# Chunk-selecting attention and a squared-ReLU feed-forward layer on one core: the first token tile of every batch taken ahead of the rest, the rest in parts of two and three tiles, and the order written as named steps

## Chip, cores and metric

The kernel runs on one core of one Trainium2 chip. The metric is the device time of one execution in microseconds, as the median of several runs. Everything below about times comes from those runs or from one profiled execution of the kernel before.

## The reference, cut to what matters

Inputs are q, k and v of shape (4 batches, 8 heads, 768 tokens, 64), and the weights `moe_w_in` (512 x 2048) and `moe_w_out` (2048 x 512), all in float32. Keys are grouped in 24 chunks of 32 tokens.

```python
k_min, k_max = min and max of each chunk of k, by element
ub = np.sum(np.maximum(q * k_min, q * k_max), axis=-1)   # per query and chunk
ub = np.where(causal, ub, -1e9)
top_chunks = the 6 chunks with the largest ub
scores = q @ k.T / 8, where the key's chunk is selected and key <= query, else -1e9
attn = softmax(scores); out = attn @ v
x = out with heads side by side, 3072 x 512
h = np.maximum(x @ w_in, 0.0)
return h * h @ w_out                                     # 3072 x 512
```

A query in the first 128 tokens has at most four causal chunks, so for this tile the choice of six selects all of them.

## The kernel before, in words

Everything is computed in bf16 with float32 accumulation. The work is cut into 32 slots: `slots` runs over batch, half of the sequence (384 tokens, three tiles of 128) and head pair. "A" below is the first half of a batch (`half == 0`) and "B" the second. For each slot a fixed set of steps is issued:

- `step_P` makes `qr`, the negative and positive part of the transposed queries (VectorE), and for some slots the chunk minima and maxima (`extrema`; for later halves `step_K` does it once for all head pairs with a chain of halving minima or maxima).
- `step_U` multiplies `qr` by the chunk extrema (`kbd`) on TensorE to get the bounds `ub`, finds the six largest with `nc.vector.max`, and writes `nsel`, a mask of chunks not selected.
- `step_V` transposes `nsel` and copies it into the free half of the rows of `qc`. The keys hold a one-hot code of their chunk times -2^24 in the matching rows, so one matmul of 128 rows gives scores with unselected chunks pushed far down.
- `step_E` does the score matmuls (`ps`, L358) and the exponential on ScalarE (`e`, L363); a select on GpSimd (L367) clears the part above the diagonal.
- `step_F` multiplies by v with a column of ones (`po`, L383), takes the reciprocal and writes `x`.

After a half has all its `x`, `step_X` transposes it (on TensorE or with DMA transposes) and puts that half's feed-forward work in `queue`: 16 "ups" (`ffn_up`: four matmuls of 128x384 into `ph`, a ReLU on ScalarE or VectorE into `ht`, a square on VectorE into `h`) and 12 "downs" (`ffn_down`: four matmuls of 128x512 into `py`; after the fourth down of a tile, a copy to `ob` and a store). `fill` takes items from `queue` between the attention steps, by a quota for each slot. The order of all instructions is the order in which the Python code issues them (`manual_schedule`); each engine works through its own list in that order.

Batch 0's first half is special. Its q and k are staged in float32 in 16 DMAs, cast, and transposed on TensorE (`step_cast`, `step_T0`); no feed-forward work exists until `step_X(0, True)`. Its second half and batch 1's first half are transposed on TensorE in `step_T1` and placed by DMA (`place`); later halves use DMA transposes (`tr`). Loads that cast to bf16 are issued from GpSimd (`load_n`, `load_s`, `load_v`, `load_w`, `load_wo`) at slots listed in `later`.

The PSUM pools that matter: `psS` with 3 buffers (scores), `psF` with 2 (`ph`), `psY` with 1 (`py`), `psA` with 2 (`ub`, `qt`, `po`, `pt`).

Of the kernel before, what the change touches and what calls it, by code (L numbers as in the profile page):

```python
# [15 lines left out]

CH = 32
TOPK = 6
HT = 3
HB = HT * 128  # L20
NEG = -1.0e9
OFFSEL = -float(2 ** 24)

BANKS = (
    (((0, 0, 0, 3), (384, 2, 2, 1)), ((256, 1, 1, 2),)),
    (((0, 3, 3, 3), (384, 5, 5, 1)), ((0, 0, 3, 2), (256, 4, 4, 2)),
     ((0, 0, 5, 1), (128, 1, 3, 3)), ((0, 2, 3, 3),)),
)  # L30


@with_exitstack
def kernel(
# [12 lines left out]
    NT = S // 128  # L47
# [4 lines left out]
    NFI = DFF // 128  # L52
    scale = 1.0 / (D ** 0.5)
# [8 lines left out]
    vn = [consts.tile([128, H, NT, D + 1], BF16, tag=f"vn{i}", name="vn") for i in range(2)]  # L62
# [3 lines left out]
    QROW = (D, 0)  # L66
    SROW = (0, D)
    kcs = [[consts.tile([128, NP, S], BF16, tag=f"kc{i}_{h}", name="kc") for h in range(2)]
           for i in range(2)]
    qcs = [consts.tile([128, NP, 2, HB], BF16, tag=f"qc{i}", name="qc") for i in range(2)]  # L70


    qn0 = consts.tile([128, HT, NP, 4, D], BF16, tag="qn0", name="qn")

    nsel = [consts.tile([128, HT, 2, D], BF16, tag=f"ns{i}", name="nsel") for i in range(3)]
    kbds = [consts.tile([128, NP, 2, 2, NC], BF16, tag=f"kbd{i}", name="kbd")
            for i in range(2)]
# [3 lines left out]
    def load_n(n, b, j):  # L81
        t = nat[n, b, j] = work.tile([128, DM], BF16, tag=f"{n}n", bufs=7, name=f"{n}n")
        nc.gpsimd.dma_start(  # L83
            out=t.rearrange("p (h d) -> p h d", d=D),
            in_=(q if n == "q" else k)[b, :, 128 * j:128 * (j + 1)]
            .rearrange("h p d -> p h d"))

    def load_s(n, b, half):

        t = nat[n, b, half] = work.tile([128, H, HT, D], BF16, tag=f"{n}s", name=f"{n}s")  # L90
        nc.gpsimd.dma_start(
            out=t.rearrange("p h j d -> p h (j d)"),
            in_=(q if n == "q" else k)[b, :, HB * half:HB * (half + 1)]
            .rearrange("h (p j) d -> p h (j d)", j=HT))

    def load_v(b, h0, h1, j0, j1):
        if j1 - j0 == 1:
            nc.gpsimd.dma_start(
                out=vn[b % 2][:, h0:h1, j0, 0:D],
                in_=v[b, h0:h1, 128 * j0:128 * j1].rearrange("h p d -> p h d"))  # L100
        else:
            nc.gpsimd.dma_start(
                out=vn[b % 2][:, h0:h1, :, 0:D],
                in_=v[b, h0:h1].rearrange("h (j p) d -> p h j d", p=128))


    staged = []

    def stage(p, pool):
        t = []  # L110
        for eng, src in ((nc.sync, k), (nc.scalar if p < 2 else nc.sync, q)):
            x = pool.tile([128, HT, 2, D], F32, tag=f"st{len(t)}", bufs=NP, name="stage")
            for hh in range(2):
                eng.dma_start(
                    out=x[:, :, hh, :],
                    in_=src[0, 2 * p + hh, 0:HB].rearrange("(j p) d -> p j d", p=128))
            t.append(x)
        staged.append(t)

    ctx.enter_context(tc.manual_schedule())  # L120
    early = ExitStack()
    epool = early.enter_context(tc.tile_pool(name="early", bufs=NP))
    for p in range(NP):
        stage(p, epool)
# [3 lines left out]
    cmask = consts.tile([128, HT, 2, NC], BF16, tag="cmask", name="cmask")  # L128
    nc.vector.memset(cmask, 0.0)
    ident = consts.tile([128, 128], BF16, tag="ident")  # L130
    make_identity(nc, ident)
# [4 lines left out]
    for g in range(4):  # L136
        nc.gpsimd.affine_select(
            out=cmask[g * 32:(g + 1) * 32], in_=cmask[g * 32:(g + 1) * 32],
            compare_op=ALU.is_ge, fill=NEG,
            base=12 + g, channel_multiplier=0,  # L140
            pattern=[[4, HT], [0, 2], [-1, NC]])

    hmask = consts.tile([128, 2, 2, 12], BF16, tag="hmask")
    nc.vector.memset(hmask, 0.0)
    for r in range(2):
        nc.vector.memset(hmask[64 * r:64 * r + 64, 0, r, :], -1.0)
        nc.vector.memset(hmask[64 * r:64 * r + 64, 1, r, :], 1.0)

    nc.vector.memset(qn0[:, :, :, 0, :], 0.0)
    nc.vector.memset(qn0[:, :, :, 3, :], 0.0)  # L150
    nc.vector.memset(vn[0][:, :, :, D:D + 1], 1.0)

    for h in range(2):
        nc.vector.tensor_copy(
            kcs[0][h][SROW[h]:SROW[h] + D, :, 0:HB],
            oneh[:, 0:HB].unsqueeze(1).to_broadcast([D, NP, HB]))
    warm = consts.tile([128, 1], F32, tag="warm")
    nc.scalar.activation(warm, hmask[:, 0, 0, 0:1], ACT.Exp)

    def codes(i, p, c0):  # L160
        for h in range(2):
            nc.sync.dma_start(
                kcs[i][h][SROW[h]:SROW[h] + D, p, c0:S], oneh[:, c0:S])

    def clear(i):
        nc.vector.memset(nsel[i][:, :, :, 12:D], 0.0)
        if i == 0:
            nc.vector.memset(vn[1][:, :, :, D:D + 1], 1.0)
# [4 lines left out]
    def col_of(half, j, i):  # L173
        for n, bank in enumerate(BANKS[half]):
            for (at, jj, i0, m) in bank:
                if jj == j and i0 <= i < i0 + m:
                    return 512 * n + at + 128 * (i - i0)
        raise KeyError

# [3 lines left out]
    kbd = {}  # L183


    def step_cast(p):
        t = staged[p]
        kst = work.tile([128, HT, 2 * D], BF16, tag="kst", name="kst")
        nc.vector.tensor_copy(kst.rearrange("p j (h d) -> p j h d", h=2), t[0])
        nc.scalar.copy(qn0[:, :, p, 1:3, :], t[1])  # L190
        st[p] = {"kst": kst}

    def extrema(kt, s):

        b, half, p = slots[s]
        km = work.tile([128, 2, 12], BF16, tag="km", name="km")
        kv = kt.rearrange("p (c j) -> p c j", j=CH)
        nc.vector.tensor_reduce(km[:, 0, :], kv, axis=AX.X, op=ALU.min)
        nc.vector.tensor_reduce(km[:, 1, :], kv, axis=AX.X, op=ALU.max)
        nc.vector.tensor_mul(  # L200
            kbds[b % 2][:, p, :, :, 12 * half:12 * half + 12], hmask,
            km.unsqueeze(2).to_broadcast([128, 2, 2, 12]))

    def step_T0(s):

        p = s
        t = st[s]
        tk = psF.tile([128, HB], BF16, tag="ph", name="tk")
        tq = psF.tile([128, HB], BF16, tag="ph", name="tq")
        for j in range(HT):  # L210
            nc.tensor.matmul(tk[:, 128 * j:128 * (j + 1)], lhsT=t["kst"][:, j, :],
                             rhs=ident, is_transpose=True, start=True, stop=True)
# [11 lines left out]
    def step_T0b(s):  # L224
        nc.scalar.copy(kcs[0][1][0:D, s, 0:HB], st[s]["tk"][D:128])
# [437 lines left out]
```

## Time and profile before

| | |
|---|---|
| median of 3 runs | 285.89 us (285.44 to 286.31) |
| profiled execution, its own time | 286.44 us |
| profiled execution, span from first to last instruction | 284.7 us |
| TensorE (PE) busy | 258.8 us, 91% of the span, 2360 matmuls |
| weight loads (PEld) | 159.8 us, 56% |
| VectorE (DVE) busy | 170.0 us, 60% |
| ScalarE (ACT) busy | 179.9 us, 63% |
| GpSimd (POOL) busy | 83.9 us, 29% |
| mean granted TensorE clock | 0.981 |
| DMA | 33.32 MB in 105423 packets, mean 117 GB/s |

Busy time of TensorE is the time in which at least one matmul was under way. It includes the filling and draining of the pipeline, so a stretch can be shown as fully busy while fewer columns pass than the engine could take. The table is a mean over stages with different limits; the prediction reads it stage by stage.

### The profile page before, as it was taken

The page shows a single profiled execution, that of the slowest core. Times are in us where ns is not written, and L with a number is a line of the kernel's source. Part 1 is how long each engine was busy: PE and PEld are TensorE (multiplying, and loading weights), DVE is VectorE, ACT ScalarE, POOL GpSimd, SP SyncE. Part 2 cuts the span into 40 slices and gives each one's busy share as a digit, 9 for nine tenths or more (in the row PEclk, how much of TensorE's full clock was granted, in tenths as well). Part 3 has the DMA queues.
Part 4 walks back from the last instruction along what each step waited for, and adds up shares of the span by engine and source line. Part 5 has one row for each costly group of instructions (what it writes and reads, how often), then busy time and mean ns, then how long its engine had stood idle before and what let it go on. Part 6 is the DMA issues. An engine that isn't in the chain of part 4 may idle for free.

```text
span 284.7 us, 6484 instructions
## 1 busy us (share of the span) xinstructions
PE 258.8 (91%) x2360; PEld 159.8 (56%) x2360; DVE 170.0 (60%) x639; ACT 179.9 (63%) x370; POOL 83.9 (29%) x125
## 2 busy tenths in 40 slices
PE   1768779987988999999999999999999999999994
PEld 1546456644655566664565566655555666555543
DVE  6767688746797566744775377644865453342321
ACT  4586678765865777765668577756767677534410
POOL 8445131544155115721461116610211011000000
PEclk9975999999999999999999999999999999999999
DMA  8999999999999555995699629995424010101002
GB/s 158 173 217 179 219 202 166 165 173 157 92 132 177 57 96 67 194 166 129 78 202 106 119 60 122 187 165 127 122 78 58 37 39 0 39 37 39 37 37 74
DMA packets 105423, 33.32 MB, mean 117 GB/s; under 512 B 90928, under 2 KB 101424, under 8 KB 105392
## 3 DMA queue, kind: packets, MB, share of 16 engines
q0 software_dynamic: 63264, 12.85, 62.4%
q1 hardware_dynamic: 40528, 19.67, 32.4%
q10 hardware_dynamic: 1600, 0.39, 0.6%
q8 instruction: 18, 0.29, 0.4%
q14 instruction: 13, 0.11, 0.1%
HBM read 27.26 MB, written 6.29 MB: 118 GB/s over the span
## 4 chain that ended last, share of the span: by engine, by line
PE 74%; DVE 8%; ACT 7%; DMA 5%; issue 2%; SPq 1%; POOL 1%; ACTq 0%; POOLq 0%
PE py L457 26%; PE ph L438 25%; PE ps L358 11%; PE po L383 7%; DMA stage<-in_q_dram 4%; ACT ht L445 2%; ACT e L363 2%; DVE h L447 2%; PE ub L308 2%; DMA xT<-x 1%; PE tkq L260 1%; DVE x L393 1%; ACT qc L345 1%; PE qt L339 1%; ACT ob L464 1%
## 5 line engine op out<-in xcount | busy, mean ns | idle before, releaser
L363 ACT ACTIVATE e<-ps 128x512 bf16<-128x512 f32 x192 | 96.9, 549 | 24.9 <-PE ps L358 23.4
L438 PE MATMUL ph<-xT,w_in 128*128 128x384 bf16 x512 | 101.6, 325 | 2.6 <-DVE ht L443 0.8
L457 PE MATMUL py<-w_out,h 128*128 128x512 bf16 (+1 forms) x400 | 98.6, 371 | 3.8 <-DVE h L447 3.0
L447 DVE TENSOR_TENSOR h<-ht 128x384 bf16<-128x384 bf16 x128 | 47.8, 377 | 73.0 <-ACT ht L445 72.5
L445 ACT ACTIVATE ht<-ph 128x384 bf16<-128x384 f32 x120 | 59.0, 494 | 40.8 <-PE ph L438 38.8
L367 POOL TENSOR_SCALAR_AFFINE_SELECT e<-e 128x384 bf16<-128x384 bf16 x64 | 33.6, 526 | 157.4 <-ACT e L363 157.4
L438 PEld LDWEIGHTS <-w_in 128*128 128x128 bf16 x512 | 47.2, 97 | 32.8 <-issue 4.7
L358 PE MATMUL ps<-qc,kc 128*128 128x384 bf16 (+2 forms) x320 | 58.7, 287 | 2.5 <-DVE qc L334 1.0
L457 PEld LDWEIGHTS <-h 128*128 128x128 bf16 x400 | 37.0, 98 | 35.9 <-DVE h L447 6.4
L358 PEld LDWEIGHTS <-kc 128*128 128x128 bf16 x320 | 27.6, 100 | 18.1 <-issue 2.4
L383 PEld LDWEIGHTS <-e 128*128 128x128 bf16 x672 | 26.5, 100 | 6.9 <-POOL e L367 1.9
L383 PE MATMUL po<-vn,e 128*128 128x65 bf16 x672 | 28.3, 196 | 1.3 <-POOL e L367 1.2
L315 DVE MAX8 m<-ub 128x8 f32<-128x24 f32 (+1 forms) x160 | 16.6, 171 | 8.4 <-PE ub L308 8.3
L464 ACT COPY ob<-py 128x512 f32<-128x512 f32 x19 | 11.3, 593 | 11.5 <-PE py L457 11.3
L393 DVE TENSOR_TENSOR x<-po,r 128x384 bf16<-128x384 f32 x32 | 17.8, 558 | 1.1
L308 PE MATMUL ub<-kbd,qr 128*128 128x48 bf16 (+1 forms) x160 | 9.8, 182 | 4.0 <-ACT qr L218 1.6
L83 POOL DMA_DIRECT2D kn<-in_k_dram x15 | 13.3, 886 | 0.3 <-issue 0.3
L83 POOL DMA_DIRECT2D qn<-in_q_dram x15 | 13.3, 889 | 0.0
L344 DVE COPY qc<-qt 64x384 bf16<-64x384 bf16 (+1 forms) x28 | 8.9, 317 | 6.9 <-PE qt L339 6.9
L265 ACT COPY tT<-tkq 128x768 bf16<-128x768 bf16 x8 | 11.6, 1449 | 2.1 <-PE tkq L260 2.0
L283 DVE TENSOR_TENSOR km<-km 128x384 bf16<-128x384 bf16 (+3 forms) x40 | 11.6, 291 | 1.4
L308 PEld LDWEIGHTS <-qr 128*128 128x128 bf16 x160 | 7.6, 98 | 6.3 <-ACT qr L218 2.5
(67 smaller groups left out, 173.4 us busy)
## 6 DMA issues: line engine op xcount, KB each, us to landing
out_dram<-ob SPq DMA_DIRECT2D x23, 256.0 KB, 2.3
vn<-in_v_dram POOLq DMA_DIRECT2D x6, 384.0 KB, 8.9
w_in<-in_moe_w_in_dram POOLq DMA_DIRECT2D x2, 1024.0 KB, 11.5
w_out<-in_moe_w_out_dram POOLq DMA_DIRECT2D x2, 1024.0 KB, 12.5
kn<-in_k_dram POOLq DMA_DIRECT2D x15, 128.0 KB, 5.6
qn<-in_q_dram POOLq DMA_DIRECT2D x15, 128.0 KB, 7.0
kc<-tT SPq DMA_DIRECT2D x10, 192.0 KB, 6.0
qc<-tT SPq DMA_DIRECT2D x10, 192.0 KB, 7.4
```

Of the source, the lines that this page charges most:

```text
L83: nc.gpsimd.dma_start(out=t.rearrange("p (h d) -> p h d", d=D), in_=(q if n == "q" else k)[b, :, 128 * j:128 * (j + 1)] .rearrange("h p d ...
L308: nc.tensor.matmul(ub[:, j - j0], lhsT=st[s]["qr"][:, w, 128 * j:128 * (j + 1)], rhs=kbds[b % 2][:, p, w, :, 0:ncs], start=False, stop=(j ...
L315: nc.vector.max(out=m8[:, j, hh, :], in_=ub[:, j - j0, hh, :])
L358: nc.tensor.matmul(ps[:, at:at + 128 * m], lhsT=kcs[b % 2][hh][:, p, 128 * j:128 * (j + 1)], rhs=qcs[half][:, p, hh, c:c + 128 * m], start ...
L363: nc.scalar.activation(e[:, 512 * n + lo:512 * n + hi], ps[:, lo:hi], ACT.Exp, scale=float(scale))
L367: nc.gpsimd.affine_select(out=d, in_=d, compare_op=ALU.is_ge, fill=0.0, base=0, channel_multiplier=-1, pattern=[[0, 3], [1, 128]])
L383: nc.tensor.matmul(po[:, hh, i, :], lhsT=t["e"][hh][:, c:c + 128], rhs=vn[b % 2][:, 2 * p + hh, j, :], start=(j == 0), stop=(j == iq))
L393: nc.vector.tensor_mul(x[:, :, 128 * p:128 * (p + 1)].rearrange("p j (h d) -> p h j d", h=2), po[:, :, :, 0:D], r.to_broadcast([128, 2, HT ...
L438: nc.tensor.matmul(ph[:, 0:HB], lhsT=w_in[:, ki, 128 * f:128 * (f + 1)], rhs=xT[:, ki, :], start=(ki == 0), stop=(ki == NKI - 1))
L445: nc.scalar.activation(ht, ph[:, 0:HB], ACT.Relu)
L447: nc.vector.tensor_mul(h, ht, ht)
L457: nc.tensor.matmul(py[t][:, n0:n1], lhsT=h2[hb, f][:, 128 * t:128 * (t + 1)], rhs=w_out[:, f, n0:n1], start=(f == 0), stop=(f == NFI - 1))
```

## The change

The token tiles of a batch are no longer split 3 + 3. The first tile (tokens 0 to 127, called z here) is taken for all four batches at the very beginning and without any selection: the steps `z_cast`, `z_T`, `z_E`, `z_F`, `z_X` compute plain causal attention for it, with matmuls over 64 rows and a triangle of -2^24 (`tri`) added by a matmul. The rest of a batch is a part A of two tiles and a part B of three (`T0`, `NTP`). The feed-forward work has ten blocks instead of eight: two blocks of two z tiles each, then A and B of each batch. An up of a z or A block has matmuls of 256 columns, one of a B block 384.

A part A slot has three exponentials instead of four, because both heads share banks (`BANKA`); a part B slot keeps its eight. The q and k of batch 0 are loaded with whole groups of tokens contiguous per partition (`load_p`, and `stage` for the z tiles), and are transposed by `spread`: sixteen matmuls of 64 columns against pieces of the identity. Later halves still use DMA transposes (`tr`).

Feed-forward work is chosen by `pick` from two lists, `ups` and `downs`, that run over all blocks: a down is taken when its four `h` are at least five items old, and ups and downs alternate; at most 37 `h` tiles are alive (`HCAP`). `fill` spends a budget of columns per slot. The order of the steps is written as text: `PRELUDE` before the slots, and for each kind of slot a line of `SLOTS`. Names: `f` spends a share of the budget on ups or downs, `fu` on ups alone, `up.n` spends n x 512 columns on ups, `idle.n` does n matmuls whose result nobody reads, `go` issues the DMAs that are due, `KB` and `K` are the extrema, `T` a batch-0 transpose.

```diff
-HT = 3
-HB = HT * 128
+T0 = (1, 3)
+NTP = (2, 3)
+HCAP = 38
+BANKA = ((0, 2, 2, 1), (128, 1, 1, 2), (384, 0, 1, 1))
+PRELUDE = """
+up.2 cast.0 idle.6 castv.0 load.k.0 zT.0 idle.3 up.2 cast.1 load.q.0 zE.0 wi.0 zT.1 stage.q.2
+castv.1 stage.k.2 idle.2 zE.1 zK.0.1.0 zF.0 zK.0.1.1 wi.1 wi.2 vz.2 up.2 stage.k.3 zX.0
+T.0.k.1.S.a T.0.k.0.S.a zF.1 stage.q.3 idle.2 zX.1 T.0.q.1.S.a T.0.q.0.S.a place.0 cast.2 codez
+codes.0 K.0.1 placez P.0 K.0.0 zT.2 vz.3 up.2 idle.2 zE.2 cast.3 U.0 up.1 wi.3 zT.3 V.0.a up.2
+zE.3 loadv.0 zF.2 zF.3 load.k.1 up.3 zX.2 up.2 loadv.1 load.q.1 up.1 zX.3 wo.0 wo.1 P.1 codes.1
+"""
+SLOTS = {
+    "A00": "fu E.0 fu P E.1 fu U fu fu E.2 fu go V.a fu fu fu T.1.k.1.S.v T.1.k.2.S.a",
+    "A01": "E.0 go fu F.0 F.1 E.1 U fu T.1.k.0.S.a E.2 V.a P T.1.q.0.S.v fu T.1.q.1.S.a",
+    "A02": (
+        "fu fu fu fu E.0 KB.0 F.0 F.1 fu T.1.q.2.S.a E.1 place.1 U go V.a fu E.2 KB.1 fu "
+        "P fu fu"),
+    "A03": "fu fu fu E.0 up.1 up.1 E.1 F.0 U F.1 V.v E.2 fu P fu go",
...
+    "A": "F.0 f E.0 F.1 f f E.1 go U f E.2 f V.a f K P f",
...
+    "B": "E.0 f f E.1 F.0 E.2 go.2 f f E.3 E.4 E.5 U go f F.1 f f E.6 E.7 V.v f K P f",
+}
+BUDGET = {"A": (13860, 13200, 11000, 11550), "B": (8000, 8000, 8000, 8000)}
+TAIL = (5000, 2000)
...
+    def spread(x, src, r0):
+        for r in range(8):
+            for h in range(2):
+                nc.tensor.matmul(
+                    x[D * h:D * h + D, r, :], lhsT=src[:, D * (r0 + r):D * (r0 + r + 1)],
+                    rhs=iv[:, :, h, :], start=True, stop=True)
+    def z_E(b):
+        e = st["z", b] = work.tile([128, 1920], BF16, tag="e", bufs=4, name="e")
+        for h in range(2):
+            ps = psS.tile([128, NP, 128], F32, tag="ps", name="pz")
+            nc.tensor.matmul(ps, lhsT=ident, rhs=tri.unsqueeze(1).to_broadcast([128, NP, 128]),
+                             start=True, stop=False)
+            for p in range(NP):
+                nc.tensor.matmul(
+                    ps[:, p, :], lhsT=ktz[D * h:D * h + D, b, p, :],
+                    rhs=qz[D * h:D * h + D, b, p, :], start=False, stop=(p == NP - 1))
...
+    def z_F(b):
+        for i in range(H):
+            c = 512 * (i % 2) + 128 * (i // 2)
+            nc.tensor.matmul(po[:, i, :], lhsT=e[:, c:c + 128], rhs=vz[:, b, i, 0:D],
+                             start=True, stop=True)
+            nc.tensor.matmul(su[:, i:i + 1], lhsT=e[:, c:c + 128], rhs=vz[:, b, i, D:D + 1],
+                             start=True, stop=True)
...
+        if kb < 3 and f % 3 == 1:
+            nc.vector.tensor_scalar_max(ht[:, 0:w], ph[:, 0:w], 0.0)
+        else:
+            nc.scalar.activation(ht[:, 0:w], ph[:, 0:w], ACT.Relu)
...
+    def pick(kind="ud"):
+        can_u = bool(ups) and "u" in kind and live[0] < HCAP - 1
+        can_d = False
+        if downs and "d" in kind:
+            kb, t, c = downs[0][:3]
+            need = [made.get((kb, f)) for f in range(4 * c, 4 * c + 4)]
+            if all(need):
+                lag = count[0] - max(x[1] for x in need)
+                can_d = lag >= 5 or not can_u
+        if can_d and (since[0] >= 1 or not can_u):
+            x = downs.pop(0)
+            ffn_down(*x)
...
+    def fill(cols, kind="ud"):
+        credit[0] += cols
+        while credit[0] > 0:
+            c = pick(kind)
+            if not c:
+                credit[0] = 0
+                break
+            credit[0] -= c
```

Counted from the two programs as they are issued: TensorE has 512 up matmuls of 384 columns before, and 256 of 384 and 384 of 256 after, so the same number of columns; the downs are the same 196,608 columns. ScalarE does 192 exponentials before and 184 after, and 120 ReLUs before (all of 384 columns) against 145 after; VectorE does 128 squares before and 160 after.

## The prediction

> **What bounds the kernel now.** I read the page's busy times and slices first, then the busy time by stages, then the chain of waits for what one instruction costs when they follow without a gap, and last the timeline of VectorE for the costs there.
>
> ```profile
> span 284.7 us, 6484 instructions
> ...
> PE   1768779987988999999999999999999999999994
> ...
> PEclk9975999999999999999999999999999999999999
> ```
>
> TensorE is busy nearly all the time after the first quarter. Its granted clock was half between about 18 and 28 us (slices 3 and 4), then full to the end. Next, busy time by stages; I cut at the first score matmul of each half (A0, B0, A1, B1, A2, B2, A3, B3, the number being the batch). Columns: stretch, its length, then busy us of PE, PEld, DVE, ACT, POOL, granted clock, DMA share, GB/s.
>
> ```profile
> 0.00:9.30 9.30, 2.63 (x23) 2.06 (x24) 6.21 (x25) 3.76 (x7) 8.07 (x16) 1.00 1.06 161
> 9.30:32.20 22.90, 18.16 (x184) 12.40 (x183) 16.71 (x62) 15.52 (x32) 9.01 (x14) 0.78 1.56 196
> 32.20:66.90 34.70, 30.80 (x358) 20.11 (x359) 24.51 (x85) 25.92 (x45) 13.94 (x18) 1.00 1.47 175
> 66.90:93.20 26.30, 23.19 (x214) 13.99 (x212) 21.47 (x84) 17.12 (x37) 10.21 (x15) 1.00 1.32 141
> 93.20:123.80 30.60, 30.40 (x316) 19.70 (x314) 19.59 (x79) 23.71 (x50) 12.33 (x16) 1.00 1.21 108
> 123.80:152.10 28.30, 26.94 (x222) 15.55 (x219) 17.17 (x72) 17.26 (x39) 9.56 (x14) 1.00 1.31 147
> 152.10:185.20 33.10, 32.77 (x331) 20.92 (x328) 20.36 (x81) 24.80 (x52) 12.26 (x16) 1.00 1.09 114
> 185.20:213.20 28.00, 26.77 (x222) 15.63 (x219) 16.91 (x72) 17.33 (x39) 4.30 (x8) 1.00 0.80 125
> 213.20:284.70 71.50, 67.09 (x522) 39.39 (x518) 27.11 (x85) 34.47 (x72) 4.16 (x8) 1.00 0.14 39
> ```
>
> Busy time does not say how much of TensorE's pace is used, so I take intervals from the chain of waits (start, length, what), where matmuls follow each other:
>
> ```profile
> 126.18 1.26 SPq L418
> ...
> 127.49 3.45 DMA xT<-x
> ...
> 135.73 0.22 PE ps L358 x2
> ...
> 245.25 0.86 PE py L457 x4
> 246.11 0.65 PE ph L438 x4
> 246.76 0.96 PE po L383 x30
> ...
> 250.75 0.67 PE pt L411 x12
> ```
>
> So a matmul takes 0.215 us for 512 columns, 0.163 for 384, 0.11 for 256, 0.056 for 128, 0.032 for 65. Counting every matmul of a stage at these prices gives TensorE's least time, the "floor". Before: start to A0's end 10.7 of 32.2 us, B0 29.0 of 34.7, A1 21.5 of 26.3, B1 30.3 of 30.6, A2 26.1 of 28.3, B2 32.7 of 33.1, A3 26.1 of 28.0, B3 with the tail 66.3 of 71.5. Sum 242.6 of 284.7. The later B halves run at TensorE's pace within 0.4 us; 42 us are lost, 21.5 of them before 32 us, where no feed-forward work exists (its first matmul is at 29.2 us), 5.7 in B0, some 9 in the A halves (the 4.7 us of SP's queue and DMA transpose at 126 us are such a place: no feed-forward work is left until the half's x is transposed), some 5 at the tail.
>
> **The change, from batch 1 to the end.** The program order gives the columns issued per stage. Before, 38,912 of the 393,216 feed-forward columns are issued before A1; after, 68,608, because the z blocks exist early. The rest, 324,608 columns at 0.163/384 = 0.4245 ns, is 137.8 us. Attention of a part A slot: six score matmuls of 128 or 256 columns for two heads and two more of 128, 0.55; weights 10 x 0.032; bounds and transposes 0.24; together 1.1 us. Of a part B slot: scores 1.63, weights 30 x 0.032, bounds and transposes 0.38, together 3.0. Three batches of four and four: 49; transposes of the last x 0.7. Floor 187.5 us (24.3 for an A part, 26.9 for a B part, 60.8 for the last B part with the tail), against 202.9 before.
>
> What is lost on top: the list of ups still holds 13 items when the transpose of the next x starts, so that wait should vanish; I keep 0.8 us for each of three A parts. In part B the order puts `V.v` close before the next slot's `E.0`; the mask's transpose and two copies of 0.35 take about 1 us, under two shares of 889 columns (0.75 us): 0.3 us a slot, 2.7 in all. The tail is built as before: 4.9. Sum 197.5 us, against 217.8 in the trace. ScalarE would be at 5.2 of 5.8 us in the tightest part B slot (exponentials at 0.485 apart: two in 1.08 with the last one's drain), so it doesn't take over. The halving of `h` tiles into 256 columns costs 32 more ReLUs and squares, about 0.28 us of ScalarE and 0.2 of VectorE each, hidden under TensorE there.
>
> **The change, the start.** Here nothing is hidden, and VectorE sets the pace. Its prices from the timeline (start, length, what):
>
> ```profile
> 4.18 0.47 DVE L189 CAST kst<-stage 128x384 bf16<-128x384 f32 x1 [0.33 <-DMA stage<-in_k_dram]
> ...
> 25.34 0.64 DVE L315 MAX8 m<-ub 128x8 f32<-128x24 f32 x6
> ...
> 102.09 0.56 DVE L393 TENSOR_TENSOR x<-po,r 128x384 bf16<-128x384 f32 x1
> ...
> 106.49 1.14 DVE L283 TENSOR_TENSOR km<-km 128x384 bf16<-128x384 bf16 x4
> ```
>
> Scaled by elements, the prelude asks of VectorE: four casts 0.48, four evictions of 512 float32 0.6 (between 0.47 for the cast and the 0.69 of the row for `ob`), two extrema chains of the z keys 1.5 and two of part A 1.9, four times reciprocal and x 0.8, four copies of the transposed x 0.33, bounds, mask, qr and the first eight squares and three ReLUs about 4: near 18.5 us. The first staged tile landed at 4.18 us before; it is larger now (256 KB in long runs against 96 KB), so I keep 4.2. Summed without a gap this would be 22.7; followed by hand, cast, 32 narrow matmuls, eviction, scores, exponential, weights, x, for two batches, then the A extrema, then two more batches, the last transpose of x comes at 28 to 31. The narrow matmuls (64 columns) have no row: from 0.023 (the bounds, 24 columns) to 0.056; 288 of them, 6.6 to 16 us, nearest to the half-width transposes of `tkq` (six in 0.19): 8 us, most of it under VectorE. The 15 idle matmuls cost 3.2 us in gaps; on the path they would cost that. I take 28.5 for the prelude.
>
> Part A of batch 0: its first two slots hold 24 ups of four 256-column matmuls and need 14.6 us of TensorE; with the alternation of two `ph` buffers 15.6. The third slot is bound by VectorE (two extrema chains, 5.6 us) and the fourth by its chain of bounds, mask and copies, 3.1. Together 24.3. Part B of batch 0: floor 26.9; the second slot's extrema of three batches give VectorE 7.9 us against 6.4, so 1.5 more, and 1 for waits: 29.5. GpSimd's loads are 12.25 MB of float32 until the last of `w_out`, 11.8 before, where it landed at 53.3 us; the first down stands at about 53, so I let the loads cost nothing; each us that they are late there is a us. Two GpSimd copies of v stand ahead of the `w_in` loads and wait for the staged v; at 0.5 (the 384-wide select's 526 ns) to 1.5 us each they delay loads first used at about 21 us, so nothing. On SP, part A's `place` is issued near 20 us and takes 6 to 7 (its like before), just ahead of 28.5.
>
> Start 82.3 against 66.9: the start is 15.4 us longer, the rest 20.3 shorter. Span 279.8. The profiled run's own time was 1.74 us over its span, and the median 0.55 under that, so 1.2 is added: **281.0 us**.
>
> **Rivals.** (1) Slower: the prelude is one serial chain and runs like the old start. There the measured time stood to the busiest engine's least time as 1.46 (9.3 to 6.4, VectorE) and 1.54 (22.9 to 14.8), and 1.18 in B0; on 20.1, 22.3 and 28.4 that is 29.3 + 34.3 + 33.5 = 97. With 197.5 and 1.2: 295.8. It decides from a start of 87 us on. For it: in-order engines with a chain over three of them. Against it: part of the old 1.54 is the half clock, under which that stretch's 9.6 us floor was 19.2. Chance 0.19.
>
> (2) The chains overlap and the start needs only its engines: 4.2 + 18.5 + 22.3 + 28.4 = 73.4; with 195 behind it and 1.2: 269.6. Chance 0.14.
>
> (3) The clock. In the third and fourth slot of batch 0's part A TensorE has 3.7 us of work in 8.7. If the clock drops to half there for the 10 us that the trace shows it at half, the 8 us of work of that fourth slot and the next take 16, less the slack of 3: 5 us, 286, no change. No stretch of the trace after 29 us has so little TensorE work, and the clock stayed full. The Trainium skill, "TensorE: Matmul & The Clock Gate", section "HAM oscillation — how this bites in real kernels", says that a gap without matmuls of over about 3.4 us sends the clock back to half; it speaks against this change. The trace neither bears it out nor refutes it, having no such gap after 29 us. Chance 0.09.
>
> (4) Later B parts do not keep pace: one `py` buffer with only downs in the last two slots of each B part (the cap on `h` leaves no ups there), so each fourth down waits for ScalarE, 0.5 to 1 us; with a full V chain, 0.7 us more for each of 11 slots: 289. For it: before, four downs in a row stand only at B0's end and in the tail, and B0 is where 5.7 us are lost. Against it: score and weight matmuls stand between most downs. Chance 0.08.
>
> **The numbers.** My forecast has 0.50, with its own range 275 to 287. A measurement here can tell about 0.3%, 285.0 to 286.75. Faster: 0.46 of the forecast, (2), and 0.02 of (3): 0.62. Within: 0.03, and 0.05 of (3): 0.08. Slower: 0.01, 0.02 of (3), (1), (4): 0.30. The range from 270 to 293 takes in (2) but for a little and most of (1).
>
> **What would show it.** In the profile after: first up matmul near 21 us; first score matmul of part A of batch 0 (the first read of `kz`) near 28.5; batch 1's part A beginning at 82 (87 or more means (1), 75 means (2)); no DMA wait for `xT` in the chain; PEclk 9 from the third slice on, a 5 or so near 45 to 55 us meaning (3); spacing of part B slots 6.8 us. If batch 1 begins by 84 and the end is still above 286, my sum for the rest is wrong.

## The result: 303.4 us, six per cent slower, and the profile after

The changed kernel takes 303.39 us (302.38 to 305.19, four runs) against 286.1 (285.44 to 286.31) in the same comparison: ratio 1.0615, interval 1.0554 to 1.0676. The forecast was 281.0, range 270 to 293. Medians here take in all executions; ratios leave out those that took over 1.5 per cent longer than the fastest of the same kernel.

The page of the kernel after, in the same lines as before:

```profile
span 303.5 us, 7258 instructions
...
PE   3967488849999999999999699999999999999994
...
PEclk9979699966999999999999899999999999999999
```

TensorE's row falls to 4 twice in the first nine slices (of 7.6 us each), the second time where part A of batch 0 ends; the clock's row is below 9 in slices 3, 5, 9, 10 and 23. Busy time by stages, same columns as the prediction's table: prelude, A0, B0, A2 and the end:

```profile
0.00:40.90 40.90, 26.15 (x366) 16.41 (x367) 19.79 (x80) 15.14 (x28) 16.36 (x27) 0.87 1.22 187
40.90:69.60 28.70, 22.45 (x292) 16.95 (x291) 23.38 (x94) 15.33 (x37) 9.40 (x15) 0.89 1.26 155
69.60:100.40 30.80, 29.33 (x304) 18.38 (x303) 19.31 (x83) 19.63 (x39) 7.14 (x11) 0.94 0.82 92
...
153.40:182.70 29.30, 26.69 (x228) 17.36 (x225) 17.20 (x75) 16.98 (x40) 11.99 (x18) 0.94 1.30 139
...
235.80:303.50 67.70, 62.49 (x522) 38.78 (x519) 23.58 (x85) 37.73 (x81) 4.17 (x8) 0.99 0.12 36
```

| stage | forecast | after | excess |
|---|---|---|---|
| prelude, to the first score matmul of batch 0's part A | 28.5 | 40.9 | 12.4 |
| A0 | 24.3 | 28.7 | 4.4 |
| B0 | 29.5 | 30.8 | 1.3 |
| batch 1 to the end | 197.5 | 203.1 | 5.6 |
| span | 279.8 | 303.5 | 23.7 |

Three quarters of the miss (18.1 of 23.7 us) lie before batch 1, over half in the prelude alone. The chain of waits (start, length, what) shows two kinds of DMA waits:

```profile
1.67 7.77 DMA zst<-in_v_dram
...
15.20 20.71 DMA vz<-in_v_dram
...
102.75 1.26 SPq L551
...
108.46 6.38 DMA tT<-kn
```

The first two are the prelude: staged v, then v of the fourth z tile, which lands 20.7 us after its issue. The last two are part A of batch 1, where the DMA transposes of the next k stand behind those of x on SP's queue; the same pair returns at 161.65 (7.86 us) and 217.68 (6.52 us). VectorE's timeline shows when the prelude can begin (in brackets its idle time before, and what ended it):

```profile
7.36 0.43 DVE L243 CAST zb<-zst 128x512 bf16<-128x512 f32 x1 [4.64 <-DMA zst<-in_k_dram]
...
10.93 0.43 DVE L243 CAST zb<-zst 128x512 bf16<-128x512 f32 x1 [1.72 <-DMA zst<-in_k_dram]
...
35.68 0.21 DVE L291 RECIPROCAL r<-su 128x8 f32<-128x8 f32 x1 [4.96 <-PE su L286]
```

The first tile of k is cast at 7.4 us and the second at 10.9, not at 4.2; and VectorE, which was to set the pace, stands still for 5 us at 31 us.

### The profile page after: what moved, and what is told of

It reads as the page before. It is cut to its first block, busy times and chain, and to the rows that moved or that the text cites. A ratio compares the mean times of both kernels' runs of the same rounds, so it can differ in the third digit from the quotient of the medians.

```text
span 303.5 us, 7258 instructions
## 1 busy us (share of the span) xinstructions
PE 271.9 (90%) x2747; PEld 177.2 (58%) x2747; DVE 172.2 (57%) x724; ACT 180.6 (60%) x389; POOL 86.8 (29%) x137
## 4 chain that ended last, share of the span: by engine, by line
PE 60%; DMA 16%; DVE 11%; SPq 6%; ACT 2%; POOL 2%; issue 2%; DVEq 0%; ACTq 0%
PE py L591 21%; PE ph L569 19%; PE ps L424 10%; DMA tT<-kn 7%; DMA vz<-in_v_dram 7%; PE po L506 5%; DVE km L352 4%; SPq L551 3%; SPq L328 3%; DMA zst<-in_v_dram 3%; DVE h L578 2%; PE qt L408 1%; PE ub L390 1%; ACT ht L576 1%; DVE ht L574 1%
## 5 line engine op out<-in xcount | busy, mean ns | idle before, releaser
L569 PE MATMUL ph<-xT,w_in 128*128 128x256 bf16 (+1 forms) x640 | 102.5, 295 | 3.5 <-ACT ht L576 1.1
L578 DVE TENSOR_TENSOR h<-ht 128x256 bf16<-128x256 bf16 (+1 forms) x160 | 52.0, 327 | 59.8 <-ACT ht L576 56.1
L576 ACT ACTIVATE ht<-ph 128x256 bf16<-128x256 f32 (+1 forms) x145 | 61.9, 433 | 32.2 <-PE ph L569 29.5
L463 ACT ACTIVATE e<-ps 128x512 bf16<-128x512 f32 (+1 forms) x128 | 66.9, 575 | 18.5 <-PE ps L424 18.4
L428 POOL TENSOR_SCALAR_AFFINE_SELECT e<-e 128x256 bf16<-128x256 bf16 (+1 forms) x64 | 30.4, 475 | 146.2 <-ACT e L463 80.1
L424 PE MATMUL ps<-kq 128*128 128x128 bf16 (+2 forms) x224 | 48.1, 286 | 1.0 <-ACT kq L413 0.7
L446 ACT ACTIVATE e<-ps 128x512 bf16<-128x512 f32 (+1 forms) x48 | 25.1, 526 | 19.5 <-PE ps L424 19.5
L424 PEld LDWEIGHTS <-kq 128*128 128x128 bf16 x224 | 20.0, 99 | 13.6 <-DVE kq L413 3.0
L424 PE MATMUL ps<-kq,kz 128*128 128x128 bf16 (+1 forms) x128 | 27.6, 238 | 0.0
L598 ACT COPY ob<-py 128x512 f32<-128x512 f32 (+1 forms) x24 | 13.6, 568 | 19.6 <-PE py L591 19.5
L397 DVE MAX8 m<-ub 128x8 f32<-128x24 f32 (+1 forms) x160 | 16.6, 170 | 14.5 <-PE ub L390 14.4
L506 PE MATMUL po<-vz,e 128*128 128x65 bf16 x160 | 23.0, 195 | 0.0
L352 DVE TENSOR_TENSOR km<-km 128x384 bf16<-128x384 bf16 (+5 forms) x80 | 20.1, 251 | 2.8
L514 DVE TENSOR_TENSOR x<-po,r 128x256 bf16<-128x256 f32 (+1 forms) x32 | 15.7, 491 | 1.1
L144 POOL DMA_DIRECT2D kn<-in_k_dram x15 | 13.3, 890 | 0.9 <-issue 0.6
## 6 DMA issues: line engine op xcount, KB each, us to landing
w_in<-in_moe_w_in_dram POOLq DMA_DIRECT2D x4, 512.0 KB, 15.6
```

The costliest lines, as they stand in the source:

```text
L352: nc.vector.tensor_tensor(y, x[:, :, :, 0:m], x[:, :, :, m:2 * m], op=op)
L397: nc.vector.max(out=m8[:, j, hh, :], in_=ub[:, j, hh, :])
L424: nc.tensor.matmul(ps, lhsT=kt, rhs=kq_of(b, half)[:, hh, p, 1, c:c + 128 * m], start=True, stop=True)
L428: nc.gpsimd.affine_select(out=d, in_=d, compare_op=ALU.is_ge, fill=0.0, base=0, channel_multiplier=-1, pattern=pattern)
L446: nc.scalar.activation(e[:, 512 * n:512 * n + w], ps[:, 0:w], ACT.Exp, scale=float(scale))
L463: nc.scalar.activation(e[:, 512 * n + lo:512 * n + hi], ps[:, lo:hi], ACT.Exp, scale=float(scale))
```

## The experiments

All times below are medians unless said otherwise; the kernel before ran beside each group at 285.1 to 286.9 us, and no kernel here is faster than it. One table first, from the traces, one execution of each kernel (us; k1 is the cast of the second staged k tile; e1, e2, e8 and e12 are told in their sections):

| kernel | k1 cast | first score | k1 to score | A0 | B0 | rest |
|---|---|---|---|---|---|---|
| after | 10.9 | 40.9 | 30.0 | 28.7 | 30.8 | 203.1 |
| e3_idle | 11.6 | 41.3 | 29.7 | 28.0 | 29.0 | 202.5 |
| e4_tr_early | 11.0 | 44.5 | 33.5 | 28.1 | 30.4 | 197.7 |
| e5_no_w | 11.5 | 42.4 | 31.0 | 32.0 | 29.9 | 200.1 |
| e6_no_v | 11.3 | 43.3 | 32.0 | 28.4 | 30.0 | 199.9 |
| e7_no_w_no_v | 11.2 | 39.7 | 28.5 | 30.2 | 29.3 | 200.8 |
| e9_put | 12.9 | 40.8 | 27.9 | 28.4 | 30.8 | 200.4 |
| e10_put_vz | 12.4 | 42.7 | 30.3 | 28.2 | 30.9 | 201.1 |
| e11_all | 15.9 | 45.6 | 29.7 | 28.2 | 29.7 | 197.9 |
| e13_put_warm | 11.8 | 40.8 | 29.0 | 28.3 | 29.8 | 202.6 |
| e14_quiet | 12.4 | 42.1 | 29.7 | 29.1 | 30.7 | 201.8 |
| e15_quiet_warm | 11.8 | 39.6 | 27.7 | 28.8 | 29.6 | 201.8 |
| e16_best | 11.7 | 42.2 | 30.5 | 27.5 | 29.3 | 197.5 |
| e17_quiet_warm_kq | 15.5 | 44.1 | 28.6 | 29.1 | 30.0 | 202.7 |
| e18_best_kq | 14.4 | 41.8 | 27.4 | 27.5 | 29.3 | 197.5 |

The first score is noisy. The kernels after, e3 and e4 have the same prelude, instruction by instruction, and reach it at 40.9, 41.3 and 44.5 us. What moved is the landing of v of the fourth z tile, at 35.9, 35.2 and 39.5 (one line of the chain of each, in this order):

```profile
15.20 20.71 DMA vz<-in_v_dram
...
15.86 19.34 DMA vz<-in_v_dram
...
15.28 24.21 DMA vz<-in_v_dram
```

So this landing ends the prelude of the changed kernel, 5 to 6 us before the first score, and differences of less than 3.6 us in that column tell nothing.

### Earlier v: e1 and e2

e1 loads v of the first two z tiles by a casting DMA, without GpSimd's copy; e2 issues vz.2 and vz.3 ahead of two quarters of w_in.

```diff
e1: -castv.0 ... castv.1    +vz.0 ... vz.1       (stage("v", ...) removed)
e2: -wi.1 wi.2 vz.2 ... vz.3    +castv.1 vz.2 vz.3 ... wi.1 wi.2
```

> Change: the v of the first two z tiles is no longer staged in float32 and cast by GpSimd; it is loaded by a casting DMA like that of the other two, so GpSimd's queue isn't held until the staged v lands (9.5 us). Theory A (the order of the loads sets the start): the first casting load is issued near 3 us instead of 10.05, every later load lands 4 to 7 us earlier, the wait for vz before z_F of batches 2 and 3 (3.7 us) shrinks to under 1, batch 1's part A begins at 92 to 96 us instead of 100.4, the time is 295 to 299. Rival B (the chain over the engines sets the start): begins at 98 to 101, time 301 to 304.

> Change: the two casting loads of v for the z tiles of batches 2 and 3 are issued ahead of the second and third part of w_in. Theory A: TensorE's wait for vz at 31 to 36 us (4.1 us) goes, w_in lands 2 us later and its first use hides that; part A of batch 0 begins at 36.5 to 38 instead of 40.9, time 299 to 300. Rival B: the wait moves to another link of the chain (evictions, squares), under 1 us gained, time 302.5 to 304.

e1: 310.58 us, ratio 1.0796 (1.0711 to 1.0881), slower than after where 295 to 299 was expected. The load of vz.1 was issued at 6.1 us and landed at 26.3; behind it the placing of the z keys took 13.8 us (36.0 to 49.8), and the first score came at 48.8, waiting for the codes, with this placing just behind. e2: 306.76 us, ratio 1.0673 (1.0601 to 1.0746), no gain where 299 to 300 was expected. In e2's traced execution (926 us, left out of the ratio) TensorE ran at a quarter of its pace throughout, 0.84 us for 512 columns, so that only its landings are read: vz.2 and vz.3 came at 25 us instead of 35. If they landed so in the other executions too, which no trace shows, the wait named in the chain went and the time stayed; something else would end at nearly the same moment.

### Two terms settled: e3 and e4

```diff
e3: +idle.5, idle.5, idle.3 in slots A02 and A03 (26 idle matmuls)
e4: -at(s0 - 6 + i // 3 + half, load_n, ...)    +at(s0 - 7 + (i // 3 + half) // 2, load_n, ...)
    -at(s0 - 4 + i // 3, tr, ...)               +at(s0 - 5 + i // 3, tr, ...)
```

> Change: 26 further matmuls of 512 columns that nobody reads, in the third and fourth slot of batch 0's part A, where TensorE has little to do. Theory C (the half clock at 63 to 73 us costs time): the granted clock stays full there, batch 0's part B takes 27.5 to 28.5 us instead of 30.8, the time is 300 to 301.5. Rival D: the 5.6 us of extra matmuls stand in the path as much as they save, time 303 to 306, clock full all the same.

> Change: from batch 1 on, the DMA transposes of the next part are issued one slot earlier, and the loads that they read one or two slots earlier, so that they no longer stand behind the transposes of x on SP's queue. Theory E (the excess of 5.6 us over the forecast after batch 1's start is the wait for these transposes and the clock drop that follows): the third slot of each part A falls from 6.8, 10.3 and 7.0 us to 6.0 to 6.3, the time is 297.5 to 300. Rival F (TensorE's order itself): those slots stay within 0.5 us, time 302.5 to 304.

e3: 303.63 us, ratio 1.0513 (1.0432 to 1.0595). In after the granted clock is half from 63.1 to 73.3 us; in e3 it is full from 41.4 us to the end (page):

```profile
PEclk9999879999999999999999999999999999999999
```

B0 goes from 30.8 to 29.0, its first slot from 8.54 to 6.72. The clock cost about 2 us there. The median of all four executions does not show it, and the ratio (1.0513 against 1.0615) leaves it open, since the intervals overlap. e4: 301.97 us, ratio 1.0524 (1.0467 to 1.0581), above the 297.5 to 300 that was expected. The rest takes 197.7 us, the forecast's 197.5; part A of batch 2 as an example (columns as above):

```profile
155.60:181.00 25.40, 24.70 (x223) 16.73 (x224) 16.58 (x75) 17.01 (x40) 9.41 (x15) 1.00 1.15 146
```

It was 29.3, and the third slots take 6.3 to 6.4 us, near the 6.0 to 6.3 expected. The gain behind batch 1's start is 5.4 us in the trace; the whole span fell by 2.8 (303.5 to 300.7), because in this execution e4's prelude came 3.6 us later. The median fell by 1.4.

### Fewer loads: e5, e6, e7

```diff
e5: -wi.1 wi.2 ... wi.3     lhsT=w_in[:, ki, 128 * (f % 4):128 * (f % 4 + 1)]
e6: -vz.2 vz.3 loadv.0 loadv.1     z tiles read vz[:, b % 2]; batch 0's slots read vz
e7: both
```

> Leaves out the loads of the last three quarters of w_in; every up multiplies by the first quarter. Nothing else moves. Theory L (the start is bound by the time of the 16 DMA engines: by 40.9 us the trace of after shows 12.7 us of each engine spent on w_in's 2048 packets and 14.9 us on the 5604 packets of 128 bytes of v): three quarters of w_in are 9.5 us that stood ahead of vz.2 and vz.3, so these land near 25 to 27 us instead of 34.8 and 35.9, the first score matmul of part A comes at 32 to 35 us instead of 40.9, and the total is near 296. Theory S (the prelude is a serial chain over VectorE, ScalarE and TensorE that takes 40 us whatever the loads do): first score matmul at 39 to 41 us, total 301 to 304.

> Leaves out the loads of v with 128-byte packets in the start (vz.2, vz.3, and both of batch 0's parts; the z tiles of batches 2 and 3 and batch 0's slots read the staged v instead); all of w_in is loaded. Theory L with the price by packet: 14.9 us of each DMA engine go, first score matmul of part A at 28 to 32 us, total 290 to 294. Theory L with the price by byte: these packets are 1.4 MB of 12 MB read by then, 3.7 us at 390 GB/s, first score matmul at 36 to 38 us. Theory S: 39 to 41 us, total 301 to 304.

> Both: neither the last three quarters of w_in nor the 128-byte loads of v in the start. This leaves the chain of the engines alone, so it tests the 28.5 us that the prediction worked out for the prelude, plus about 3 us for k staged at 7.4 instead of 4.2 us. Theory L: first score matmul of part A at 28 to 32 us, no half clock before it after 28 us, part A of batch 0 in 24 to 27 us, batch 1 at 84 to 88 us, total 288 to 292. Theory S: first score matmul at 38 to 41 us, batch 1 at 97 to 100.

306.27, 304.20 and 302.15 us; first score at 42.4, 43.3 and 39.7, not the 28 to 35 of the theory that DMA volume binds. But the runs do not decide about volume, for what is left out is replaced: in e7 w_out was issued at 14.3 us instead of 39.5, and from 10 to 40 us the DMA moved 187, 208 and 214 GB/s in steps of 10 us, against 217, 216 and 180 in after. Small transfers waited meanwhile. Chain of e7:

```profile
10.38 10.70 DMA kn<-in_k_dram
...
30.89 10.85 DMA kz<-ktz
```

Part A's k, half a megabyte, takes 10.7 us (7.9 in after, but 10.7 too in e4, whose prelude is that of after), and the placing of the z keys, a transfer within SBUF, 10.85.

### Later z tiles: e8

The z steps of batches 2 and 3 move into the slots A00 and A01, their loads behind w_in and v.

```diff
-PRELUDE: stage.q.2 ... zX.3 of batches 2 and 3
+SLOTS["A00"]: cast.2 zT.2 cast.3 zE.2 zT.3 zE.3   SLOTS["A01"]: zF.2 zF.3 zX.2 zX.3
```

> Nothing left out. The z tiles of batches 2 and 3 (staging, casts, transposes, scores, v) are moved out of the prelude into the first two slots of part A of batch 0, and their loads behind w_in and v of batch 0; batch 0's part B transposes move one slot later. Theory L: what part A needs comes sooner in the queue, first score matmul at 32 to 35 us; part A of batch 0 takes on some 3 us of VectorE work, 30 to 32; batch 1 at 93 to 97, total 296 to 299. Theory S: the z steps moved away are 10 us of chain, first score matmul at 29 to 31, and part A as much longer: batch 1 at 99 to 101, total 302 to 304, no change.

319.58 us (312.5 to 322.6, the traced execution 322.6), slower than after in every execution. In the trace the first score came at 39.9 us, little sooner, and the first slot of part A took 21 us: the staged tiles, now last in SP's queue, landed at 46.8. Both theories had the saving too large and the price too small.

### No DMA ahead of part A's operands: e9 to e12

```diff
e9:  -place.0 ... placez    +put.0.0.0 put.0.1.0 put.0.0.1 put.0.1.1 ... putz    codez codes.0 first
e10: e9, vz.2 vz.3 ahead of wi.1
e11: e10, castv on VectorE ahead of zF, and e4's lines
e12: e9 without the loads that e7 leaves out
```

> Nothing left out. In the start, the DMAs that place batch 0's q, k and z keys into the score operands (place.0, placez) become copies on ScalarE and VectorE, and the DMAs of the chunk codes are issued first on SP. Theory M (what part A waits for is the landing of small transfers of SP's queue, 8 to 11 us each while GpSimd's loads fill the DMA engines; in the lean run the keys' transfer was issued at 30.9 and landed 10.85 us later, just ahead of the first score matmul): with all loads kept, vz.2 and vz.3 still land at 35 to 36 us and stand ahead in TensorE's order, so the first score matmul of part A is only 0 to 3 us sooner, 38 to 41 us; total 300 to 303. Theory S (serial chain over the engines): the four to six added copies lengthen it, 41 to 43 us, total 303 to 306.

> As e9_put, and the loads vz.2 and vz.3 are issued ahead of w_in's second and third quarter. Theory M: both waits ahead of part A are gone, first score matmul at 32 to 35 us; then w_in's last quarter and the k of part B come as late as before (about 40 and 47 us), so part A of batch 0 gives 2 to 4 us back: batch 1 at 94 to 97, total 296 to 300. Theory S: 40 us or more, total 302 to 305.

> As e10_put_vz, and the copies of the staged v are VectorE's, after the first z scores, so that GpSimd's loads begin at about 5 us instead of 10; and the DMA transposes of later halves are issued one slot sooner, as in e4_tr_early. Theory M: the loads end some 4 us sooner, first score matmul at 30 to 34 us, batch 1 at 88 to 94, the rest 198: total 288 to 294. If earlier loads only delay the staged tiles, as when v came by casting DMAs: batch 1 at 97 to 101, total 296 to 300.

> Leaves out what e7_no_w_no_v leaves out (three quarters of w_in, the 128-byte loads of v in the start), and has the copies of e9_put instead of place.0 and placez. No landing of a DMA is left between the casts of the z tiles and part A except q and k of part A themselves. This is the chain of the engines that the prediction put at 28.5 us for the prelude, with the first staged tile 3.2 us later. Theory M: first score matmul at 29 to 33 us against 41.9. Theory S: 40 us or more.

302.86, 303.34 and 303.41 us, and for e12 302.47 and 308.68 in its two executions, the slower one traced. e9 came out as its theory M said; e10 came out as the rival, theory S, said, and so did e12's first score; e11 met neither of its ranges. In e12's trace the first ups waited for w_in's quarter, which landed at 31.7 us, 19.1 after its issue, and the score came at 46.8. In e10 no DMA is left in the chain between 12.4 us and the first score, and that still comes at 42.7. Its windows show the clock at half (last three columns: granted clock, DMA share, GB/s):

```profile
20.00:30.00 10.00, 6.29 (x87) 3.72 (x84) 7.50 (x27) 5.67 (x10) 1.10 (x2) 0.50 1.60 190
30.00:40.00 10.00, 9.77 (x107) 6.17 (x106) 4.42 (x15) 4.43 (x9) 4.00 (x5) 0.50 1.57 170
```

The chain of e9 shows what stands there:

```profile
28.83 0.85 PE dm L655 x2
29.69 0.43 PE pz L268
...
36.22 0.33 PE pz L271 x4
```

TensorE, nearly without a gap, and until 35.3 us at half clock: an idle matmul of 512 columns takes 0.43 us instead of 0.215, and four of 128 columns take 0.54 until 35 us and 0.33 after it. In e11 GpSimd's loads begin at 2.8 us, q lands at 15.9 instead of 19.3 in e10, and the second k tile is late in exchange: 15.9 instead of 12.4.

### Traffic and clock: e13, e14, e15

```diff
e13: e9 with idle.16 for idle.6, and idle.4, idle.4, idle.8, idle.3 in TensorE's gaps
e14: e12 with load.k.1, load.q.1, wo.0, wo.1 moved behind part A's first scores
e15: e14 with the idle matmuls of e13
```

> As e9_put, with 29 more idle matmuls in the gaps that TensorE has in e9_put's trace before 27 us. Nothing left out. Theory H (with the DMA waits gone the start is a gapless chain of TensorE at half clock: e9_put's trace has TensorE busy without a gap from 26.5 to 40.8 us, of that at half clock until 35.3): if the clock stays full after 18 us, the 8.8 us at half become 4.4, and some 1.5 us go between 18 and 26; first score matmul of part A at 34 to 36 us instead of 40.8, total 294 to 298. Theory M (the landings of loads): 39 to 42 us whatever the clock, total 301 to 304.

> As e12_put_lean, with the loads of w_out and of part B's q and k moved behind the first scores of part A, so that before them only the staged tiles, part A's q and k, the codes and one quarter of w_in are moved. It leaves out what e12_put_lean does. The old idle matmuls only. Theory M (traffic delays what is needed): q, k and w_in land by 16 to 18 us instead of 21, 24 and 32; the first score matmul comes at 33 to 36 us if TensorE's clock is half from about 18 us on, as in e9_put, and at 29 to 31 if it is not. Theory H alone: 38 to 41 us, as in e9_put.

> e14_quiet with the idle matmuls of e13_put_warm: no competing traffic and, if they do what they are meant to, no half clock. This is the engines' chain alone, which the prediction put at 28.5 us with the first staged tile at 4.2 us; it lands 3 us later. If traffic and clock together are the cause: first score matmul at 29 to 33 us. If it stays above 36 us, the chain itself was sized too short.

303.06, 304.90 and 303.67 us; first score at 40.8, 42.1 and 39.6. In e13, which came out as its theory M said, the clock was full from 19.5 us, and TensorE waited instead for vz.3, which landed at 37.1. In e14, with little traffic (127 GB/s from 20 to 30 us and none from 30 to 40), q still landed at 21.3, and TensorE ran at half pace until 37 us. e15 cures both but for 3.4 us of half clock, and is above 36 us all the same: volume alone does not bind, and by e15's expectation the prediction's chain was sized too short. Its trace shows a landing in the path first:

```profile
1.67 8.51 DMA zst<-in_v_dram
...
10.23 0.61 POOL vz L246
...
11.57 10.82 DMA qn<-in_q_dram
...
29.54 0.61 DVE ktz L261
...
39.72 0.23 PE ps L424 x3
```

The staged v lands at 10.2 us; GpSimd copies it and only then issues part A's loads; q lands at 22.4; and 17.3 us of engine work follow with hardly a gap.

### The order of the loads: e17 and e18

```diff
e17: e15  -castv.0 load.k.0 ... load.q.0    +load.k.0 load.q.0 castv.0
e16: e13, put.* and putz moved behind zE.3, codes behind stage.q.3, with 23 of e3's 26 idles and e4's lines
e18: e16  with e17's order, and vz.2 vz.3 ahead of wi.1
```

> Nothing left out: e13_put_warm with the copies of q and k behind the z tiles' own steps (in e9_put they held ScalarE for 2 us ahead of a cast), the codes issued where after has them, the idle matmuls of e3_idle, and the DMA transposes one slot sooner as in e4_tr_early. Theory H: first score matmul at 32 to 35 us, part A of batch 0 in 28, part B in 29, the rest 198: total 288 to 293, still not faster than before. Theory M: first score matmul at 39 to 42, total 296 to 300.

> e15_quiet_warm with part A's loads of k and q issued ahead of GpSimd's copy of the staged v (at about 3 us instead of 10.8 and 11.6). It leaves out what e15_quiet_warm does. Theory K (a chain of two landings and the engines: in e15_quiet_warm's trace v lands at 10.2 us, q's load is issued behind its copy and lands at 22.4, and 17.3 us of engine work follow without a wait, though traffic and clock were cured): q lands by 16 us, k's first tile 2 to 3 us later than before, first score matmul at 33 to 36 us instead of 39.6. If the engines' chain alone is the limit from the first tile on: 39 to 42.

> Nothing left out: e16_best with the same change of order, and vz.2 and vz.3 ahead of w_in's second and third quarter. Theory K: first score matmul at 36 to 39 us instead of 42.2 (the w_in quarters land about as late as before), total 293 to 296, still not the 286.7 of the kernel before. Otherwise: 41 to 44 us, total 297 to 300.

e17: 307.51 us. q landed at 15.7 as expected, and the first score came at 44.1, outside both ranges. The chain begins elsewhere:

```profile
2.37 13.13 DMA zst<-in_k_dram
...
15.53 0.44 DVE zb L243
...
17.08 0.97 PE dm L655 x2
...
21.13 1.86 PE dm L655 x4
...
23.42 1.25 PE dm L655 x4
...
44.29 0.23 PE ps L424 x3
```

The second k tile, issued at 2.4 us as always, is pushed from 12 to 15.5 us by loads issued at 2.8 and 3.6. The Trainium skill, "DMA: Bandwidth & Descriptors", section "Issuing engines are not separate DMA queues", says that transfers from all engines run on the same 16 DMA engines and interleave; these 13.1 us against 10.0 in e14 agree with it.

e16: 298.28 us, ratio 1.0404 (1.0368 to 1.0441). e18: 297.63 us, ratio 1.0386 (1.0351 to 1.0421), the best version, still 11 us behind the kernel before. Both missed the range of the theory that they were built on (a first score at 32 to 35 and 36 to 39) and fell in or next to the other. The page of e18:

```profile
span 296.1 us, 7367 instructions
...
PEclk9859999999999999999999999999999999999999
```

Its rest is 197.5 us and its B0 29.3. What separates it from the forecast is the prelude, 13.3 us, and A0, 3.2.

## Why the prediction was wrong, point by point

**The prelude, 28.5 against 40.9: the step that failed.** It was built as the first tile's landing, 4.2, and 24.3 us of engine work beginning there, with the loads at nothing. In the kernel after, the load of v of the fourth z tile lands at 35.9, and the first score follows 5.0 later. Three parts of the step fell.

First, the landing. "The first staged tile landed at 4.18 us before ... so I keep 4.2" is wrong by size and by kind. Six transfers of 256 KB share the DMA engines, k's first tile came at 7.4 us, and what the chain needs is the second, at 10.9.

Second, "I let the loads cost nothing" and "two GpSimd copies of v ... so nothing". The wait for v held back q's load, which is on the chain of e15, and v of the last z tiles landed at 35.9. But no limit cured alone shortened the start: in e5, e6, e9, e10 and e13 the first score came at 40.8 to 43.3, where the next limit stood.

Third, VectorE as the pace. Its sum was near (18.5 forecast, though the terms named add up to 19.6; 19.79 busy), yet it works for less than half of the prelude, because its operations stand between TensorE's and ScalarE's in one chain. From the second k tile's cast to the first score, the table has 27.4 to 33.5 us, whether loads are left out, idle matmuls keep the clock up or part A's operands are copied. In e17, where no DMA wait stands in that stretch, it is 28.6, and 4.1 of them are idle matmuls at half clock (0.97, 1.86 and 1.25 us in the chain). Without these it would be 24.5, and in e18 by the same subtraction 23.3, near the 24.3 of the sum. But the sum begins with the first tile's cast, and these begin with the second's, when the cast and the eviction of the first tile's k are done (7.36 to 9.21 us in after). So, by an estimate from these figures, the work was sized 1 to 2 us short; it starts 7 to 12 us later than assumed, and in the kernels of the table something (idle matmuls, half clock, copies in place of DMAs, or a landing) adds 3 to 9 us to it. Neither figure was run: no kernel here came to its first score before 39.6 us, so which limits must go together to come near 28.5 stays open. In e1 and e12 the stretch is 39.5 and 34.2, with the long landings told above.

**Rival (1)** came true in its condition (start above 87, here 100.4) and in part in its mechanism: the start is a serial chain, but its longest link in after is the landing of a load (20.7 us), which the rival does not name. Its ratios of 1.46 and 1.54 rest on least times of 6.4 and 14.8 us that its rows do not show (VectorE 6.21 busy in the first, TensorE 18.16 in the second). For the prelude the ratio here is 40.9 to 20.1, 2.0. It put A0 at 34.3 (28.7) and B0 at 33.5 (30.8), so that its start, 97, came close by errors that cancel: luck.

**A0, 24.3 against 28.7.** Where nothing is left out or moved into part A, the four slots take 8.5 to 9.0, 8.7, 5.0 and 5.9 to 6.0 us; e1 alone has a longer first slot, 10.7, with the wait for its placing in it. The first two were put at 15.6 by TensorE; ReLUs and squares for two `ph` buffers alternate on ScalarE and VectorE in the chain there, and they take 17.2 to 17.6. That this alternation is the cause was not tested. The third was right (5.6 forecast). The fourth, 3.1, was short by half; without the clock's drop it takes 3.9 to 4.3 (e3, e16, e18), but then the third, with idle matmuls in it, takes 6.5.

**B0 and rival (3).** B0 was forecast at 29.5 and is 29.0 to 29.3 with the clock kept up, 30.8 without. The drop came in the place that rival (3) named, for the 10 us that it named, and cost 2 us instead of 5 (2.5 to 2.7 together with A0, by e3 and e18). Its premise from the Trainium skill ("TensorE: Matmul & The Clock Gate", section "HAM oscillation — how this bites in real kernels", a gap of over about 3.4 us) differs from the trace: in the 3.4 us before the drop at 63.1 the longest gap was 2.46 us, but TensorE was busy for only a quarter of them.

**The rest, 197.5 against 203.1.** The floors were right: B1 took 26.9 (floor 26.9), the whole rest 197.5 to 197.9 in e4, e11, e16 and e18. That it hits 197.5 to the tenth in e16 and e18 is luck: the three A parts are 1.0 us over their terms, B1 and B2 1.5 under, the last part 0.4 over. The wait for `xT` vanished as forecast. Missing was the next one: the same queue of SP brings the transposes of the next k, and each part A waited for these, A2 by far the longest (29.3 us against 25.3 in e4), where the clock dropped as well. The term "0.8 for each of three A parts" was the one mis-sized, and by the order of two lists: e4, which changes only when these transposes and their loads are issued, takes the excess away.

**Right besides:** the narrow transposes were cheap (32 in 0.65 us at full clock, 20 ns each, 28 forecast). The forecast priced them one after the other, by neighbours that run so. In the trace of after (49.31 us) the two that write the two halves of the partitions start 3 to 4 ns apart, and a new pair starts about every 31 ns. Rival (4) did not happen: B1 and B2 took 26.9 and 27.2 us.

## What to carry to other kernels

Time a prelude from the landing of the *last* tile that its chain needs, not of the first: add up the bytes of everything issued before that, on all queues, before adding engine work. In a start without filler work, busy sums give only a lower bound; write the chain down instruction by instruction across engines, with each DMA landing in it, and expect that curing the wait that the profile names will uncover another just behind it. Where landings set the pace, compare two executions of the same instructions before you read a difference between two kernels. When work is pulled forward to remove a late wait, look at what is next on the same queue: here the transposes of k stood behind those of x, and issuing them one slot earlier gave back all that the steady part had lost against the forecast.

## What the runs showed of the hardware

The granted clock fell to half without any long gap: before the drops at 18.7, 32.4, 63.1 and 172.3 us of the kernel after, TensorE was busy for 0.34, 0.57, 0.23 and 0.38 of the last 3.4 us, with longest gaps of 1.2 to 2.5 us. Half clock then lasted 3.4, 6.8, 10.2 and 3.4 us. In the first 10 us matmuls ran at half pace (32 narrow transposes in 1.07 us) although the granted clock was shown as full; in e14 this went on to 37 us.

Landing times in a loaded start were far from their size: v of one z tile, 0.25 MB in float32 written as bf16 in packets of 128 bytes, took 20.7 us from issue to landing, and 19.3 and 24.2 with the same instructions in e3 and e4. All packets of 128 bytes until 41 us, most of them of later v, took 43 ns each on average, 14.9 us of every DMA engine. A copy of 64 KB within SBUF took 10.9 us in e7.
